# Two attention blocks in one kernel: query blocks of 256 with output and denominator in one PSUM bank, score banks 3+2, a matmul in place of a partition all-reduce, and rearranged loads

## Chip, core, metric

The kernel runs on one core of a Trainium2 chip. The metric is the device time in microseconds (us). A profile is one separate execution, so its span differs a little from the median time. Engines: TensorE (PE; PEld are its weight loads), VectorE (DVE), ScalarE (ACT), GpSimd (POOL); SP issues the DMAs, and SPq is its queue. L392 is a line of the kernel file. The *granted clock* is the share of TensorE's full clock that the chip allowed, as the trace records it.

## The reference

Two independent attention layers over 2048 tokens with 32 heads of 32 channels, in bf16, their outputs set side by side. A is plain softmax attention. B works on four segments of 512 tokens: causal softmax inside the segment, and a memory read from the segments before it.

```python
def _A_ref(x, wqkv, wo):                        # x (1, 2048, 1024)
    q, k, v = ...                               # (x @ wqkv) split into 3 x 32 heads x 32
    p = softmax(einsum('bhqd,bhkd->bhqk', q, k) * 32 ** -0.5)
    return merge_heads(einsum('bhqk,bhkd->bhqd', p, v)) @ wo

def _B_ref(x, wq, wk, wv, wo, beta):            # 4 segments of 512
    g = sigmoid(beta)                           # one gate for each head
    for s in range(4):
        a_dot = softmax(qs @ ks^T * scale + causal mask) @ vs
        a_mem = (phi(qs) @ M) / (phi(qs) @ z + 1e-6)
        outs.append(g * a_mem + (1 - g) * a_dot)
        M, z = M + phi(ks)^T @ vs, z + sum(phi(ks))
    return merge_heads(outs) @ wo
# result: concatenate([A, B], axis=-1)
```

## The kernel before

Heads go in groups of four, since four times 32 channels fill the 128 partitions. For one query block and one tile of 128 keys a *slot* holds the scores of one head, 128 keys by 512 columns, one PSUM bank. ACT takes the exponential of two slots in one call and writes them to a ring `PT` in SBUF. PE then multiplies by V, and by a matrix of ones for the denominators ("PV"). Everything else is *side work* for PE: projections of Q, K and V ("preparation" of a group), output projections, B's memory.

The kernel plans itself. A small simulator in the program books each instruction with a cost, and the order in which it books them is the order in which each engine will run them. The real engines wait for each other by semaphores, in that fixed order. A wrong cost in the plan therefore doesn't make a wrong result, but it can make a poor order.

```python
SLOTS = [(0, 1), (2, 3)]      # score banks, two at a time
PROJ = [4, 5]                 # side work
OB, LB = 6, 7                 # outputs, denominators
...
# in Recorder.op: an operation's end in the plan
t = self.free[eng]
for d in op.deps:
    t = max(t, d.end + LAT)
op.end = t + cost
...
# in b_prep: the shift of B's exponent, one number for all 128 partitions
R.op("PE", f, ...)                                  # sums of squares of q and k
R.op("DVE", lambda e, bank=bank: e.tensor_reduce(self.cbB[b][:, 1:2], self.ps[:, bank, :], AX.X, ALU.max), ...)
R.op("POOL", lambda e: e.partition_all_reduce(self.cbB[b][:, 1:2], self.cbB[b][:, 1:2], P, bass_isa.ReduceOp.max), ..., cost=1.0)
R.op("POOL", lambda e: e.tensor_scalar(self.cbB[b][:, 0:1], self.cbB[b][:, 1:2], -SCALE, None, ALU.mult), ...)
...
# in schedule, at each step of PE's plan: scores if a bank pair is free,
# else a PV step if its exponentials are done, else a piece of side work
if ready and room and self.slot_end[bk] <= now + 0.05:
    self.emit_scores(u, n, bk)
...
if not done:
    for t in self.tasks:
        if t.req[0] == "pe" and self.satisfied(t.req, now, True):
            self.resume(t)
```

## Time and profile before

| | before |
|---|---|
| time, median of 2 runs | 1611.62 us (1604.51 to 1618.72) |
| span of the profiled run | 1628.9 us |
| ACT busy | 1239.1 us |
| PE busy | 1393.8 us, mean granted clock 0.905 |

The profiled run took 1630.61 us, 1.6% above the fastest of the two timed runs (1604.51 us). It is the only profile of before, so the losses read from it are together some 20 us larger than in a run at the median (1630.6 less 1611.6, an estimate).

First the page's table of 40 equal slices of the span (here 40.7 us each). Each digit is the busy share in tenths, and PEclk is the granted clock in tenths of full speed.

```profile
PE   1588999698999987969889998879898997789998
ACT  0228999698789973969769996478888995598970
PEclk9997999798589999979669999688989999998999
```

ACT is saturated in some stretches and starved in others, and the clock dips with it. The next fence cuts the span in three: until the first exponential of A, until the end of the last exponential, and the rest. Columns: the stretch, its length, then busy us (and instructions) of PE, PEld, DVE, ACT and POOL, the granted clock, the share of the DMA engines and GB/s.

```profile
0.00:110.60 110.60, 54.01 (x406) 25.05 (x411) 31.43 (x60) 8.26 (x10) 8.97 (x29) 0.97 0.46 105
110.60:1578.50 1467.90, 1296.64 (x10952) 423.54 (x11090) 738.83 (x1105) 1230.71 (x1240) 142.85 (x315) 0.90 0.11 27
1578.50:1628.90 50.40, 43.12 (x196) 17.76 (x198) 22.04 (x32) 0.09 (x1) 0.00 (x0) 1.00 0.19 69
```

ACT's idle time in a stretch is its length less ACT's busy time: 102.3 us at the start, 237.2 us in the middle, 50.3 us at the end. This is the ledger used below: **span = ACT busy + idle of ACT at the start + in the middle + at the end.** Next, what ACT waited for (total us, times, longest):

```profile
ACT PT L392 <- PE ps L380: 145.8, 136, 30.6
ACT PT L392 <- POOL cbB L615: 87.8, 12, 14.2
ACT E L631 <- DVE KQB L508: 55.0, 6, 18.3
ACT L345 <- DMA beta<-in_B_beta_dram: 50.0, 1, 50.0
```

And two lines of the waits of all engines. "POOL cbB L615 <- issue" is the time that GpSimd stood after issuing the all-reduce: 225.1 us in 32 times, 7.0 us each. In the other, PE waits for causal masks, which GpSimd makes too.

```profile
POOL cbB L615 <- issue: 225.1, 32, 7.6
...
PE ps L444 <- POOL PT L415: 34.6, 5, 12.0
```

What a stop of PE can do to its clock, in stretches of 4 us:

```profile
388.00:392.00 4.00, 3.86 (x51) 1.92 (x49) 0.00 (x0) 4.00 (x5) 0.38 (x1) 1.00 0.02 4
392.00:396.00 4.00, 2.71 (x42) 1.71 (x39) 3.63 (x7) 0.86 (x2) 0.00 (x0) 1.00 0.08 18
396.00:400.00 4.00, 0.30 (x1) 0.14 (x2) 3.86 (x6) 2.12 (x2) 1.09 (x3) 0.76 0.66 146
400.00:404.00 4.00, 3.98 (x27) 0.98 (x26) 0.82 (x2) 3.20 (x4) 1.46 (x3) 0.50 0.44 98
440.00:444.00 4.00, 4.00 (x29) 1.59 (x26) 0.00 (x0) 3.06 (x3) 0.00 (x0) 0.50 0.00 0
456.00:460.00 4.00, 2.95 (x32) 1.34 (x32) 2.98 (x6) 1.46 (x2) 0.53 (x2) 0.99 0.28 64
```

PE has one matmul between 396 and 400; the clock goes to 0.50 and stays there until about 456, though PE is busy for 3.98 and 4.00 of 4 us in the stretches shown, and ACT gets only 3.06 to 3.20 us of work in 4. ACT waits 4.4 us for the shift, until 397.25. PE's next matmul in order is the first projection of the next segment, and the one xB buffer is only now loaded anew:

```profile
394.90 10.39 SPq L293 DMA_TRANSPOSE xB<-in_B_x_dram  x8
...
399.70 0.63 PE L505 MATMUL ps<-xB,WB 128*128 128x512 bf16 x1 [4.92 <-DVE Ls L464]
...
786.62 0.63 PE L505 MATMUL ps<-xB,WB 128*128 128x512 bf16 x1 [4.87 <-DMA xB<-in_B_x_dram]
```

The trace puts the first of these stops down to DVE. In the program this matmul waits for two xB transposes, for weights loaded before and for a bank that DVE freed at 393.0, so xB ended the wait. At the next segment change, which begins the other 60 us of half clock (784 to 844), the trace names xB itself.

### The profile page before, as it was taken

To read this page: it belongs to the slowest core of one execution; us is meant where nothing else is said; L and a number is where in the kernel's file an instruction comes from. 1 tells how busy PE (TensorE), PEld (TensorE's weight loads), DVE (VectorE), ACT (ScalarE), POOL (GpSimd) and SP (SyncE) were. 2 spreads that over 40 slices of the span, in tenths; PEclk is the share of its full clock that TensorE was granted. 3 is DMA by queue.
4 is the path that set the end of the run, shared out by engine and by line. 5 is a ranking of instruction groups with operands and counts; after the bars stand their busy time and mean duration, and the time that the engine had idled before them with its cause. 6 is when DMAs were issued, how large, how long until landed. Compare 5 with 4: busy or idle time off the path is not lost.

```text
span 1628.9 us, 26663 instructions
## 1 busy us (share of the span) xinstructions
PE 1393.8 (86%) x11550; PEld 466.4 (29%) x11696; DVE 792.3 (49%) x1196; ACT 1239.1 (76%) x1250; POOL 151.8 (9%) x344
## 2 busy tenths in 40 slices
PE   1588999698999987969889998879898997789998
PEld 0241233223223233322223323222332232222223
DVE  0343444353255654645526754545545745463643
ACT  0228999698789973969769996478888995598970
POOL 0000001001011010100101100100101101110100
PEclk9997999798589999979669999688989999998999
DMA  8220001002011001100111101100111001310002
GB/s 167 84 47 7 14 22 39 21 14 46 14 33 27 20 21 46 27 14 21 40 27 28 26 21 27 40 13 20 30 37 33 21 1 27 97 27 7 20 30 75
DMA packets 166742, 54.17 MB, mean 33 GB/s; under 512 B 160480, under 2 KB 160480, under 8 KB 166624
## 3 DMA queue, kind: packets, MB, share of 16 engines
q1 hardware_dynamic: 166624, 52.45, 13.2%
q8 instruction: 92, 1.51, 0.4%
q14 instruction: 26, 0.21, 0.0%
HBM read 35.65 MB, written 8.39 MB: 27 GB/s over the span
## 4 chain that ended last, share of the span: by engine, by line
ACT 57%; PE 23%; issue 8%; DVE 6%; SPq 3%; DMA 2%; POOL 1%; POOLq 0%; ACTq 0%; DVEq 0%
ACT PT L392 56%; PE ps L380 6%; PE ps L444 6%; PE ps L505 5%; PE ps L710 4%; PE ps L522 3%; DVE Ls L464 2%; SPq L293 1%; SPq L306 1%; DMA beta<-in_B_beta_dram 1%; DVE outsb L717 1%; DVE Ls L454 1%; DMA out_dram<-outsb 1%; ACT E L631 1%; DVE cbB L610 1%
## 5 line engine op out<-in xcount | busy, mean ns | idle before, releaser
L392 ACT ACTIVATE PT<-ps,cbA 128x1024 bf16<-128x1024 f32 x1024 | 1050.0, 1197 | 112.9 <-PE ps L380 112.1
L380 PE MATMUL ps<-QA,KA 32*128 32x512 bf16 x2048 | 421.6, 410 | 40.3 <-ACT PT L392 15.3
L392 ACT ACTIVATE PT<-ps,cbB 128x768 bf16<-128x768 f32 (+1 forms) x192 | 175.3, 1039 | 121.7 <-POOL cbB L615 87.8
L444 PE MATMUL ps<-PT,ones 128*32 128x512 bf16 (+3 forms) x2560 | 256.0, 395 | 0.0
L464 DVE RECIPROCAL Ls<-Ls 128x128 f32<-128x128 f32 x256 | 242.2, 946 | 3.6
L380 PEld LDWEIGHTS ps<-QA,KA 32*128 32x128 bf16 x2048 | 96.9, 92 | 462.7 <-ACT PT L392 399.0
L444 PE MATMUL ps<-PT,VA 128*32 128x512 bf16 x2048 | 216.4, 413 | 0.9 <-DVE Os L455 0.4
L505 PE MATMUL ps<-xB,WB 128*128 128x512 bf16 x472 | 147.7, 417 | 53.6 <-DMA xB<-in_B_x_dram 18.2
L505 PE MATMUL ps<-xA,WA 128*128 128x512 bf16 x459 | 141.7, 405 | 29.5 <-DMA xA<-in_A_x_dram 18.9
L415 POOL TENSOR_SCALAR_AFFINE_SELECT PT<-PT 128x256 bf16<-128x256 bf16 (+1 forms) x192 | 95.2, 498 | 472.1 <-ACT PT L392 469.2
L380 PE MATMUL ps<-KQB 32*128 32x128 bf16 (+3 forms) x512 | 65.9, 335 | 50.6 <-ACT PT L392 48.2
L454 DVE COPY Ls<-ps 128x512 f32<-128x512 f32 x64 | 44.0, 687 | 107.4 <-PE ps L444 106.8
L508 DVE CAST KQB<-ps 128x512 bf16<-128x512 f32 x64 | 43.6, 681 | 102.1 <-PE ps L505 102.1
L527 DVE CAST VA<-ps 128x512 bf16<-128x512 f32 x32 | 21.8, 682 | 146.5 <-PE ps L522 146.5
L657 DVE RECIPROCAL den<-den 128x128 f32<-128x128 f32 x96 | 91.3, 951 | 2.5
L444 PEld LDWEIGHTS ps<-PT,VA 128*32 128x32 bf16 x2048 | 53.0, 93 | 129.5 <-issue 120.8
L717 DVE CAST outsb<-ps 128x512 bf16<-128x512 f32 x64 | 43.5, 685 | 84.1 <-PE ps L710 72.0
L522 PE MATMUL ps<-WA,xA 128*128 128x128 bf16 x1024 | 82.5, 231 | 0.8 <-DVE VA L527 0.8
L522 PE MATMUL ps<-WB,xB 128*128 128x128 bf16 x1024 | 79.1, 230 | 1.7 <-DVE KA L508 0.5
L444 PE MATMUL ps<-PT,VB 128*32 128x256 bf16 (+3 forms) x512 | 45.9, 356 | 35.6 <-POOL PT L415 34.6
L710 PE MATMUL ps<-WoB,OTB 128*128 128x512 bf16 x237 | 68.3, 403 | 7.8 <-DVE PKt L678 2.6
L505 PEld LDWEIGHTS ps<-xB,WB 128*128 128x128 bf16 x512 | 40.8, 101 | 107.8 <-issue 67.2
(70 smaller groups left out, 900.1 us busy)
## 6 DMA issues: line engine op xcount, KB each, us to landing
WB<-in_B_wk_dram SPq DMA_DIRECT2D x32, 256.0 KB, 2.9
WB<-in_B_wq_dram SPq DMA_DIRECT2D x32, 256.0 KB, 2.9
WB<-in_B_wv_dram SPq DMA_DIRECT2D x32, 256.0 KB, 2.9
out_dram<-outsb SPq DMA_DIRECT2D x32, 256.0 KB, 2.0
WA<-in_A_wqkv_dram SPq DMA_DIRECT2D x24, 256.0 KB, 2.9
WoB<-in_B_wo_dram SPq DMA_DIRECT2D x1, 2048.0 KB, 17.6
xA<-in_A_wo_dram SPq DMA_DIRECT2D x1, 2048.0 KB, 9.5
xB<-in_B_x_dram SPq DMA_TRANSPOSE x32, 2.8
```

The lines of the kernel that those rows point to most:

```text
L380: ins = e.matmul(o, l, r, start=True, stop=True)
L392: op = R.op("ACT", lambda e: e.activation(self.PT[:, s0:s0 + n, 0:width], self.ps[:, banks[0]:banks[0] + n, 0:width], ACTF.Exp, bias=cb, s ...
L415: mo = R.op("POOL", lambda e, ap=ap, pat=pat: e.affine_select(ap, ap, pattern=pat, compare_op=ALU.is_ge, fill=0.0, base=0, channel_multipl ...
L444: ins = e.matmul(o, l, r, start=(st == 0), stop=stop)
L454: R.op("DVE", lambda e: e.tensor_copy(self.Ls2[x][:, :], self.ps[:, LB, :]), r=[("ps", LB)], w=[("Ls", x)], cost=0.66)
L464: R.op("DVE", lambda e, cs=cs: e.reciprocal(Ls[:, cs], Ls[:, cs]), r=[("Ls", x)], w=[("Ls", x)], cost=0.9)
L505: ins = e.matmul(self.ps[:, bank, :], W[:, i, :], xsl(i), start=(i == 0), stop=(i == NI - 1))
L508: op = R.op("DVE", lambda e: e.tensor_copy(dst, self.ps[:, bank, :]), r=[("ps", bank)], w=[dkey], cost=0.66)
L522: ins = e.matmul(self.ps[:, bank, P * t:P * t + P], xsl(i, t), W[:, i, :], start=(i == 0), stop=(i == NI - 1))
L657: R.op("DVE", lambda e, cs=cs: e.reciprocal(self.den[:, cs], self.den[:, cs]), r=["den"], w=["den"], cost=0.9)
L710: ins = e.matmul(self.ps[:, bank, :], lhsT, rhs, start=(j == 0), stop=(j == NG - 1))
L717: op = R.op("DVE", lambda e, ns=ns, bank=bank, ob=ob: e.tensor_copy(self.outsb[ob][:, ns], self.ps[:, bank, :]), r=[("ps", bank)], w=[("ou ...
```

## The change

Its intent: shorter query blocks (256) let output and denominator share one bank, so that two banks fall free; one goes to the scores, where ACT and PE now work on three and two slots in turn. The all-reduce of the shift leaves GpSimd: `col_max` puts the maximum of each partition, made negative, on a diagonal, a matmul with ones copies the diagonal's values to all partitions, and DVE takes the smallest. The plan gets truer costs (a change of tiling on PE costs 0.105 us), starts side work only if it fits before the next score burst ("room"), and lets B run ahead. xA is loaded in quarters so that work can start with the first, the second segment's xB has a buffer of its own and is loaded at once, and the beta gate no longer heads DVE's queue.

```diff
-QC = 512
+QC = 256
+DRAIN = 0.105
+MM = 0.213
-SLOTS = [(0, 1), (2, 3)]
-PROJ = [4, 5]
-OB, LB = 6, 7
+SLOTS = [(0, 1, 2), (3, 4)]
+OLB = 5
+PROJ = [6, 7]
+LEAD = 1.5
...  # loads
-        for i in range(NI):
-            src = self.A_x[0][:, P * i:P * i + P]
-            R.dma(... self.xA[:, i, :], src, transpose=True),
-                  w=[("xA", i)], issue=2.3, cost=3.0)
+        for c in range(4):
+            for i in range(NI):
+                src = self.A_x[0][512 * c:512 * c + 512, P * i:P * i + P]
+                R.dma(... self.xA[:, i, 512 * c:512 * c + 512], src, transpose=True),
+                      w=[("xA", i, c)], issue=0.6, mb=0.125)
+            ...  # beta after c == 0
+        self.load_xB(1)
         R.dma(... self.WoB ...)
...  # emit_scores: each slot is two key tiles by 256 queries
...  # emit_pv: one tile of 128 keys; ones go to columns 256:512 of the same bank
...  # the shift: partition_all_reduce becomes
+    def col_max(self, bank, i, mul, out, okey):
+        dg = self.diag[i]
+        R.op("DVE", ... e.tensor_reduce(out, self.ps[:, bank, :], AX.X, ALU.max) ...)
+        R.op("DVE", ... e.tensor_scalar(dg, self.ident, out, mul, ALU.mult, ALU.mult) ...)
+        R.op("PE",  ... e.matmul(self.ps[:, bank, 0:P], self.ones, dg, start=True, stop=True) ...)
+        R.op("DVE", ... e.tensor_reduce(out, self.ps[:, bank, 0:P], AX.X, ALU.min) ...)
...  # side work in runs as long as there is room
+    def mm_run(self, mms, r, w, each, k0=1):
+        while i < len(mms):
+            room = yield ("pe", 0)
+            k = max(k0, min(len(mms) - i, int((room - DRAIN) / each)))
...  # proj_tok, the V projection, books each matmul at
+        yield from self.mm_run(mms, ..., [("ps", bank)], 0.079, 5)
...  # schedule
+                        late = max(R.free["ACT"] - self.score_cost(u, n) - DRAIN - 0.25, self.slot_end[bk])
+                        room = late - now
```

## The prediction

> **What bounds it now.** ScalarE (ACT), in quiet stretches: the windows have ACT busy 99.99 of 100 us at 200-300 and 98.64 at 900-1000, at clock 1.00. Over the span ACT is busy 1239 of 1629 us, so some 390 us are idle:
> 1. About 105 us before softmax of A runs steadily (first A exponential at 110.6 us). The timeline shows VectorE blocked to 51.5 us behind the gate of beta (ACT waited 50.0 us for that DMA), with evictions queued behind it.
> 2. About 50 us tail: last exponential ends at 1578.5.
> 3. About 235 us in the middle. In the waits, the partition all-reduce holds each B shift some 7 us ("POOL cbB from issue": 225.1 us, 32 times); 87.8 us reach ACT directly. Masks behind it are late (PE waits up to 12.0 us for POOL PT), and the three segment changes starve ACT (4 of 20 us busy at 1000-1020). After these stops the granted clock is 0.50 for up to 55 us (400-456, 792-840) although PE is busy 4.00 of 4 us, and ACT falls to about 75%. The Trainium skill ("TensorE: Matmul & The Clock Gate", What's actually happening) gives half clock after one idle window of about 3.4 us; the trace agrees. It also gives full clock after one busy window; here return took far longer.
>
> **Removed, added.** Estimates from trace durations.
> - ACT: back-to-back 1024-wide exponentials start every 0.994 us (64 in 63.63); 256 elements cost 0.213 us, so about 0.14 us is fixed. A: 1024 calls become about 832 (13 per block of 32 slots): 1018 to 991 us, -27. B about -5. New ACT total about 1180-1200 us.
> - PE, occupied time at full clock from successive starts (a switch of tiling costs about 0.1 us): a score burst 0.32 us for two heads, and with three heads of 2x256 columns about the same: 1024 to 832 bursts, -60. PV per pair of key tiles unchanged (0.46 plus switch). Longer projection runs save perhaps 40 of 107 us of switches; the shift's small matmuls add about 10. Sum about 1340 to 1250 us.
> - POOL all-reduce out of the path: removes its waits and most half-clock stretches.
> - DVE: one 0.69 us copy per 256 block instead of two per 512; the same 242 us of reciprocals; about +25 us for shifts. Not a limit.
> - Second xB buffer: segment changes hidden. Beta moved: prologue loss 105 to about 50 us. Smaller output pieces: tail 50 to about 25 us.
>
> **On the critical path.** 1190 ACT + 50 prologue + 25 tail = 1265. But in the middle PE then needs about 97% of ACT's time, so I add 85 us for semaphore latencies, late scores, and a few half-clock stretches. Predicted 1350 us, range 1270 to 1440. Chances: faster 0.97, same 0.02, slower 0.01.
>
> **What would show it.** ACT A exponentials about 832, busy near 1010-1020; ACT total near 1200 and over 87% of the span; no partition all-reduce and no ACT wait on cbB over 2 us; mean clock 0.95 or more; first A exponential by about 65 us; last one within 35 us of the end; PE busy over 88%.
>
> **What would make it wrong.** More half-clock: attention alone uses only about 60% of PE, and at 116-122 us before, a stretch of attention without side work dropped the clock. Then PE binds: 1400 or more. Or the single output bank stalls PV at each of 128 block ends behind DVE's queue. Or PE blocks in order on xA pieces in the prologue.

## More of the kernel before

Last, the DMA queue at the start (start, duration and number of the issues):

```profile
2.58 10.75 SPq L293 DMA_TRANSPOSE xB<-in_B_x_dram  x8
...
15.44 20.00 SPq L306 DMA_TRANSPOSE xA<-in_A_x_dram  x8
```

Eight transposes of 512x128 for xB took 10.75 us of the queue, and eight of 2048x128 for xA took 20.00 us.

## The result

| | before | after |
|---|---|---|
| time, median of 2 runs | 1611.62 us | 1447.13 us (1445.71 to 1448.56) |
| span of the profiled run | 1628.9 us | 1444.0 us |
| ACT busy | 1239.1 us | 1200.8 us |
| mean granted clock | 0.905 | 0.974 |
| ACT idle at the start | 102.3 us | 119.9 us |
| ACT idle in the middle | 237.2 us | 63.5 us |
| ACT idle at the end | 50.3 us | 59.8 us |

The ratio of after to before is 0.8979 (95% interval 0.8805 to 0.9154). A ratio here is the mean time of one kernel's fast runs over that of the other's of the same rounds, so it isn't quite the ratio of the medians. A later set of four runs of the same kernel gave 1446.44 us and 0.8937. The change is faster, but the range of the prediction ended at 1440 us. The same slices, now of 36.1 us:

```profile
PE   2448999999989899989898889898999999999997
ACT  0104999999999999999869879599999999999930
PEclk9669999999999999999999999999999999999999
```

From the fifth slice on ACT is nearly always full, and the clock is 0.9 or more everywhere past the start. The first three slices are nearly empty. The three stretches:

```profile
0.00:133.60 133.60, 63.02 (x493) 29.38 (x498) 41.20 (x84) 13.70 (x16) 9.48 (x25) 0.81 0.44 95
133.60:1384.20 1250.60, 1138.71 (x17733) 529.62 (x17910) 760.75 (x1271) 1187.12 (x1030) 104.68 (x186) 0.99 0.13 31
1384.20:1444.00 59.80, 49.96 (x252) 22.00 (x252) 26.28 (x40) 0.00 (x0) 0.15 (x1) 1.00 0.18 66
```

What ACT waited for; the wait for cbB is gone:

```profile
ACT PT L417 <- PE ps L405: 123.9, 28, 24.0
ACT gcol L370 <- DMA beta<-in_B_beta_dram: 36.2, 1, 36.2
ACT E L661 <- DVE KQB L547: 21.0, 1, 21.0
```

The start is *longer* than before. The DMA queue shows why:

```profile
1.92 10.51 SPq L306 DMA_TRANSPOSE xB<-in_B_x_dram  x8
...
15.57 10.95 SPq L322 DMA_TRANSPOSE xA<-in_A_x_dram  x8
...
28.67 35.48 SPq L322 DMA_TRANSPOSE xA<-in_A_x_dram  x24
64.19 11.82 SPq L306 DMA_TRANSPOSE xB<-in_B_x_dram  x8
76.06 0.59 SPq L333 DMA_DIRECT2D WoB<-in_B_wo_dram  x1
76.76 0.51 SPq L299 DMA_DIRECT2D WB<-in_B_wk_dram  x1
```

The 32 quarter transposes take 10.95 + 35.48 = 46.4 us in place of 20.0, and then come eight more for the second segment (11.8 us) and the 2 MB of WoB, all ahead of the weights of the *second B block*, issued at 76.76. PE runs in order, so it stands behind them; the first line is ACT's first exponential, the second PE's first matmuls that need those weights:

```profile
62.16 3.26 ACT L417 ACTIVATE PT<-ps,cbB 128x1152 bf16<-128x1152 f32 x3 [22.96 <-PE ps L405]
...
86.60 1.03 PE L537 MATMUL ps<-xB,WB 128*128 128x512 bf16 x2 [17.10 <-DMA WB<-in_B_wk_dram]
```

xB of the first segment had landed by 14 us, yet its first exponential comes at 62 us: A's projections of the quarters stand in front of B's in PE's program, each waiting for its quarter (30.0 us in 4 waits). In the middle the remaining gaps are of one kind, an exponential waiting for scores whose preparation is late:

```profile
732.53 5.37 ACT L417 ACTIVATE PT<-ps,cbB 128x1152 bf16<-128x1152 f32 x5 [14.30 <-PE ps L405]
...
917.19 7.42 ACT L417 ACTIVATE PT<-ps,cbA 128x1536 bf16<-128x1536 f32 x6 [16.44 <-PE ps L405]
```

At the end PE runs five output blocks of A (7.1 us each) and then the last of B (14 us), with short pauses; three of these lines:

```profile
1393.32 7.08 PE L537 MATMUL ps<-xA,OTA 128*128 128x512 bf16 x32 [0.59 <-DVE outsb L743]
1400.56 7.08 PE L537 MATMUL ps<-xA,OTA 128*128 128x512 bf16 x31 [0.16 <-DVE outsb L743]
...
1426.55 13.99 PE L537 MATMUL ps<-WoB,OTB 128*128 128x512 bf16 x63 [3.48 <-DVE OTB L511]
```

### The profile page after: what moved, and what is told of

Its sections match the earlier page's. It is cut to its first block, busy times and chain, and to the rows that moved or that the text cites. A ratio compares the mean times of both kernels' runs of the same rounds, so it can differ in the third digit from the quotient of the medians.

```text
span 1444.0 us, 40280 instructions
## 1 busy us (share of the span) xinstructions
PE 1251.7 (87%) x18472; PEld 581.0 (40%) x18656; DVE 828.2 (57%) x1393; ACT 1200.8 (83%) x1046; POOL 114.3 (8%) x211
## 4 chain that ended last, share of the span: by engine, by line
ACT 72%; PE 16%; SPq 5%; DVE 5%; DMA 1%; issue 1%; POOL 0%; DVEq 0%
ACT PT L417 71%; PE ps L537 11%; SPq L322 3%; PE ps L405 3%; PE ps L466 2%; SPq L306 2%; ACT E L661 1%; DVE OL L486 1%; DMA WB<-in_B_wk_dram 1%; DVE outsb L743 1%; DMA out_dram<-outsb 0%; DVE den L687 0%; DVE OL L476 0%; DVE SQB L636 0%; DVE cbB L564 0%
## 5 line engine op out<-in xcount | busy, mean ns | idle before, releaser
L417 ACT ACTIVATE PT<-ps,cbA 128x1024 bf16<-128x1024 f32 (+1 forms) x832 | 1012.1, 1369 | 60.3 <-PE ps L405 59.9
L405 PE MATMUL ps<-QA,KA 32*128 32x256 bf16 x4096 | 324.3, 273 | 56.3 <-ACT PT L417 44.1
L466 PE MATMUL ps<-PT,ones 128*32 128x256 bf16 (+1 forms) x4864 | 309.8, 271 | 0.0
L466 PE MATMUL ps<-PT,VA 128*32 128x256 bf16 x4096 | 270.8, 279 | 4.0 <-issue 1.8
L486 DVE RECIPROCAL OL<-OL 128x128 f32<-128x128 f32 x256 | 242.4, 948 | 5.0
L417 ACT ACTIVATE PT<-ps,cbB 128x768 bf16<-128x768 f32 (+4 forms) x179 | 174.8, 1073 | 64.6 <-PE ps L405 63.9
L437 POOL TENSOR_SCALAR_AFFINE_SELECT PT<-PT 128x256 bf16<-128x256 bf16 (+2 forms) x147 | 86.1, 596 | 1089.7 <-ACT PT L417 1088.4
L466 PEld LDWEIGHTS ps<-PT,VA 128*32 128x32 bf16 x4096 | 106.6, 94 | 133.6 <-issue 124.3
L476 DVE COPY OL<-ps 128x512 f32<-128x512 f32 x128 | 86.7, 677 | 99.9 <-PE ps L466 99.3
L466 PEld LDWEIGHTS ps<-PT,ones 128*32 128x32 bf16 x4864 | 129.3, 96 | 1.3
L743 DVE CAST outsb<-ps 128x512 bf16<-128x512 f32 x64 | 43.4, 682 | 58.2 <-PE ps L537 50.4
L405 PE MATMUL ps<-KQB 32*128 32x256 bf16 (+1 forms) x768 | 63.2, 257 | 12.1 <-ACT PT L417 8.4
L537 PEld LDWEIGHTS ps<-WB,xB 128*128 128x128 bf16 x1024 | 60.2, 100 | 18.7 <-issue 16.5
```

The source lines that it names most:

```text
L405: ins = e.matmul(o, l, r, start=True, stop=True)
L417: op = R.op("ACT", lambda e: e.activation(self.PT[:, s0:s0 + n, 0:width], self.ps[:, banks[0]:banks[0] + n, 0:width], ACTF.Exp, bias=cb, s ...
L437: mo = R.op("POOL", lambda e, ap=ap, pat=pat: e.affine_select(ap, ap, pattern=pat, compare_op=ALU.is_ge, fill=0.0, base=0, channel_multipl ...
L466: ins = e.matmul(o, l, r, start=start, stop=end, skip_group_check=True)
L476: R.op("DVE", lambda e: e.tensor_copy(self.OL[x][:, :], self.ps[:, OLB, :]), r=[("ps", OLB)], w=[("OL", x)], cost=0.66)
L486: R.op("DVE", lambda e, Lq=Lq: e.reciprocal(Lq, Lq), r=[k], w=[k], cost=0.87)
```

## The experiments

Every experiment is the kernel named with one edit, checked against the reference. Differences in us are from 1447 us of after unless another kernel is named. They go across jobs and chips: e1 to e4, e5 to e8, and e9, e10 and after again were three jobs. After itself gave 1447.1 and 1446.4 us in two jobs. The kernel before, run beside each, gave medians of 1610.9 to 1623.3 us. The ratios use fast runs only: of the kernel before some runs (1629 to 1645 us), and of e5 two of four (1545 and 1548 us), lay over 1.5% above their fastest and count as slow; every run of the other kernels was fast, and so was every profiled run but that of before (see above). Most edits also change the plan, and with it the order of PE's whole program; where that matters I compared the sequences of matmuls by shape. The ledger of the profiled runs, worked out as above:

| kernel | median us | ratio to before | start | middle | end | ACT busy |
|---|---|---|---|---|---|---|
| before | 1611.6 | 1 | 102.3 | 237.2 | 50.3 | 1239.1 |
| after | 1447.1 | 0.8979 | 119.9 | 63.5 | 59.8 | 1200.8 |
| e1 second segment later | 1422.3 | 0.8826 | 98.4 | 49.9 | 74.1 | 1200.1 |
| e2 xA in eight pieces | 1417.9 | 0.8794 | 94.4 | 52.2 | 70.5 | 1200.2 |
| e3 V booked at its time | 1410.1 | 0.8749 | 117.7 | 47.3 | 43.3 | 1201.8 |
| e4 all-reduce back | 1498.8 | 0.9299 | 125.9 | 105.6 | 62.7 | 1203.9 |
| e5 before, matmul shift | 1538.1 | 0.9502 | 94.4 | 141.9 | 49.4 | 1231.0 |
| e6 score banks 2+2 | 1532.6 | 0.9554 | 120.4 | 108.9 | 77.6 | 1226.3 |
| e7 = e1 + e2 + e3 | 1378.7 | 0.8591 | 84.4 | 46.5 | 41.7 | 1201.2 |
| e8 = e7, no standing | 1368.9 | 0.8527 | 75.6 | 43.8 | 43.3 | 1200.8 |
| e9 = e8, half of V (wrong) | 1330.2 | 0.8218 | 71.2 | 18.0 | 38.5 | 1201.3 |
| e10 = e8, lead and margin | 1358.4 | 0.8389 | 76.1 | 30.8 | 47.3 | 1202.8 |

**My first theory after the result**: three losses that add. The start is lost to a serial DMA queue and to PE standing in order behind it; middle and end are PE's side work done too late. **The rival**: PE has more work than the time holds, so that whatever is saved at the start only comes back as backlog.

### e1: the second segment's load and WoB moved out of the start

```diff
-        self.load_xB(1)
-        R.dma(... self.WoB ...)
...
+        if n == 1:              # in b_prep, behind the second B block's loads
+            self.load_xB(1)
+            self.R.dma(... self.WoB ...)
```

> The kernel after, with the second segment's eight transposes of xB and the 2 MB load of WoB moved out of the start, behind the preparation of the second B block. In the trace of after they stand in the one DMA queue before the weights of the second B block, which land at 86.6 us, and TensorE waits 17.1 us in order for them. Theory (the start is lost one for one): 17 to 24 us less, about 1424 us, first A exponential near 113 us instead of 134. Rival (TensorE has more work than the rest of the time holds, so the start only moves the backlog): under 5 us less.

Measured: 1422.27 us, 25 us less; first A exponential at 118.2 us. The start gave 21.5 us of it. The middle gave 14 us, and 14 us came back at the end. That looks like backlog moving on, but it isn't shown to be: e2 has the same shift (11 us each way), and the programs of e1 and e2 have the same sequence of matmuls, which differs from that of after. The rival's "under 5 us" is out, and e7 below repeats the test with the order almost kept.

### e2: xA in eight transposes

```diff
-        for c in range(4):
-            for i in range(NI):   ... 512x128 pieces, w=[("xA", i, c)], issue=0.6, mb=0.125
+        for i in range(NI):
+            src = self.A_x[0][:, P * i:P * i + P]
+            R.dma(... self.xA[:, i, :], src, transpose=True),
+                  w=[("xA", i, c) for c in range(4)], issue=2.5, mb=0.5)
```

> The kernel after, with xA loaded by eight transposes of 2048x128 as before in place of 32 of 512x128. In the traces the eight took 20.0 us of the queue, the 32 took 46.4 us (1.3 us each). Theory (each transpose costs the queue a time of its own, little of it by bytes): the first A exponential comes 20 to 26 us earlier and the kernel is 18 to 26 us faster, about 1423 us. Rival (bytes are what counts, or the early first quarter of xA is worth as much): within 5 us.

Measured: 1417.90 us, 29 us less, a little more than expected; first A exponential at 114.1 us. The queue in this run:

```profile
15.84 20.77 SPq L321 DMA_TRANSPOSE xA<-in_A_x_dram  x8
```

20.77 us for the same bytes that took 46.4 us in quarters. Having the first quarter early was worth less than the queue time it cost. The edit also moves the beta gate behind all of xA (ACT waits 46.3 us for it in place of 36.2).

### e3: one number of the plan

```diff
-        ... [("ps", bank)], 0.079, 5)
+        ... [("ps", bank)], 0.0575, 5)
```

> The kernel after, with one number of its scheduler changed: a 128-column projection matmul of V is booked at 0.0575 us in place of 0.079 us. The trace starts 32 of them in about 1.8 us (0.056 each); 2048 of them are over-booked by 46 us. Theory (TensorE has room in the middle, but the order of its program holds side work back, so preparations come late and output projections pile up at the end): 30 to 50 us less, of it 15 to 25 us of the tail after the last exponential (62 us in after), the rest of gaps of ScalarE in the middle. Rival (TensorE is really full): under 5 us less.

Measured: 1410.05 us, 37 us less, the largest of the three, with no instruction taken away. The end gave 16.5 us and the middle 16.2 us. The plan thought that PE had no room for side work where the chip had it. So at least this part was not lack of PE time but the order.

### e4: the all-reduce back

```diff
-        yield from self.col_max(bank, 1, -SCALE, self.cbB[b][:, 0:1], ("cbB", b))
+        ... DVE tensor_reduce, POOL partition_all_reduce, POOL tensor_scalar, as before
```

> The kernel after, with the shift of B again by the partition all-reduce of GpSimd (about 7 us of delay each, 32 times, in the trace of before). Theory of the prediction (the all-reduce made the middle loss of before, by waits of ScalarE and half-clock stretches after them): 60 us slower or more, mean clock below 0.95, ScalarE waiting over 50 us for cbB. Rival (with two blocks of lead and other work to do, the 7 us are hidden, and the gain in the middle came from the pacing and banks): under 20 us slower.

Measured: 1498.80 us, 52 us more, between the two expectations. The all-reduce stands as long as ever, 7.0 us each, but reaches ACT less often than before:

```profile
POOL cbB L650 <- issue: 224.5, 32, 7.8
...
ACT PT L417 <- POOL cbB L650: 48.0, 3, 19.1
```

42 us of the loss are in the middle; the mean clock is 0.957. One thing is untested here: the plan books the all-reduce at 1.0 us, as it does in before, while it stands 7.0. No run booked it at its time, so some of its cost may be the order and not the wait itself.

### e5: the kernel before with the matmul shift alone

The edit is the same four operations as in `col_max`, in the kernel before, for B only.

> The kernel before with one part of the change alone: the shift of B by two small matmuls and VectorE in place of GpSimd's partition all-reduce (A keeps its own, eight in all). Theory of the prediction (most of the 237 us that ScalarE idles in the middle of before come from the all-reduce and the half clock after it): 80 to 160 us faster than before, 1450 to 1530 us, mean clock 0.95 or more. Rival (putting it back into the kernel after cost only 52 us, so it is worth about that here too, and the rest of the middle loss is one-ahead preparation, segment loads and pacing): 30 to 65 us faster, about 1560 us.

Measured: median 1538.08 us (1518.77 to 1547.92) with two slow runs in it; by the fast runs the ratio is 0.9502 (0.9403 to 0.9602), 82 us less (1524.98 for 1607.14, the means of the fast runs). That is the lower edge of what my theory expected, but with two fast runs the interval (64 to 96 us) reaches down to the rival's 65. The middle went from 237.2 to 141.9 us and the clock of the whole run from 0.905 to 0.957 between the profiled runs; these two differ by more than the medians do, since both kernels spread over some 30 us from run to run. So the all-reduce, alone, is worth some 82 us in the kernel before and 52 us in the kernel after, about a third of the 237 us, most of which I had put on it and the half clock after it. The other 142 us of the middle belong to something else: e6 shows one part.

### e6: score banks 2+2

```diff
-SLOTS = [(0, 1, 2), (3, 4)]
+SLOTS = [(0, 1), (2, 3)]
```

> The kernel after with score banks 2+2 in place of 3+2, the fifth bank left idle. Theory (fewer, longer exponentials and score bursts are the gain of the banks): ScalarE busy 27 to 35 us more in 1024 calls for A, TensorE some 190 more bursts of 0.32 us, kernel 45 to 90 us slower. Rival (neither engine is tight enough for it to show): under 15 us slower.

Measured: 1532.62 us, 85 us more. ACT is busy only 25.5 us more; the rest is 45 us in the middle and 18 us at the end, where PE's side work now comes late. PE's burst for two heads takes as long as that for three. These lines of after show it: six matmuls for three heads start at 704.15 and PE's next starts at 704.48, and the four for two heads start at 710.75, PE's next at 711.07.

```profile
704.15 0.39 PE L405 MATMUL ps<-QA,KA 32*128 32x256 bf16 x6
704.48 0.29 PE L466 MATMUL ps<-PT,VB 128*32 128x256 bf16 x4
...
710.75 0.39 PE L405 MATMUL ps<-QA,KA 32*128 32x256 bf16 x4
711.07 0.29 PE L466 MATMUL ps<-PT,VA 128*32 128x256 bf16 x4
```

So 1024 bursts in place of 832 cost PE 192 x 0.32 = 61 us, an estimate from these distances; the traces have A's score matmuls busy for 399.7 us in place of 324.3. The banks were worth more than any other part tried in the kernel after. I had counted 27 us for ACT and 60 us for PE, but only ACT's part is a term of the predicted sum. e6 also has four banks to fill ahead in place of five, which I didn't separate from the number of bursts.

### e7 and e8: the repairs together, and no standing in order

e7 is e1, e2 and e3, with the queue's measured times in the plan (1.3 and 2.5 us for a transpose, and 0.45 us in place of 0.1 for most other loads). e8 adds to e7, in both projection helpers:

```diff
+        yield ("t", max(self.R.lastw[k].end for k in [wkey] + [xkeys(i) for i in range(NI)]))
         bank = yield ("bank",)
```

> The three repairs e1, e2 and e3 together (second segment and WoB later, xA in eight transposes, V booked at 0.0575 us), and the scheduler told the DMA queue's times of the trace (1.3 us a 512x128 transpose, 2.5 us a 2048x128 one). Alone they gave 25, 29 and 37 us. Theory (start and tail are separate losses that add, e1 and e2 overlapping in part): 65 to 90 us faster than after, 1357 to 1382 us. Rival (they all draw on the same slack): 1395 us or more.

> e7 and one more thing: no projection is put into TensorE's program before the scheduler expects its inputs to have landed, so that TensorE does not stand in order before a load while the first B block could go on. In the trace of after TensorE waited 30 us for xA, and the first exponential came at 62 us though xB had landed by 14 us. Theory (standing in order is part of the start's loss): the first exponential before 35 us, 8 to 20 us faster than e7. Rival (the start is bound by the queue alone): within 5 us of e7.

Measured: e7 1378.67 us, 68 us less than after. Alone the three gave 25 + 29 + 37 = 91 us, so they add only in part. The cleanest pair is e3 and e7: the two sequences of matmuls agree in 16,462 of 18,656 places, the start falls by 33 us (117.7 to 84.4), middle and end by 1 and 2, and the kernel by 31 us. So what the loads cost at the start is lost one for one, and no backlog takes it back. e8 1368.87 us, 10 us less than e7, the first exponential at 25.0 us and the first of A at 89.4 us (103.5 in e7). The expectation of e8 held.

### e9: half of the V projections left out (a wrong result)

```diff
-        mms = [(..., i == 0, i == NI - 1) for t in range(4) for i in range(NI)]
+        mms = [(..., i == 0, i == 3) for t in range(4) for i in range(4)]
```

> e8 with half of the contraction of the V projections left out, a wrong result on purpose: 1024 of 2048 matmuls of 128 columns, 57 us of TensorE spread over the whole run, ScalarE's work the same. Theory (past the start, TensorE's work fills the time: the 44 us of ScalarE's gaps in the middle and the 43 us of tail are its backlog): 35 to 57 us faster than e8. Rival (ScalarE and the waits between the two set the pace): under 15 us faster.

Measured: 1330.24 us, 39 us less than e8 (of another job), for 57 us (an estimate, 1024 x 0.056) of PE's work taken out; the result is wrong. ACT did the same work. Here are the middle stretches of e8 and of e9:

```profile
89.40:1320.10 1230.70, 1174.29 (x18005) 534.99 (x18004) 774.40 (x1296) 1186.88 (x1036) 106.38 (x192) 0.99 0.14 34
85.00:1290.30 1205.30, 1103.36 (x16907) 486.61 (x17100) 776.27 (x1299) 1187.29 (x1038) 107.18 (x194) 0.98 0.15 35
```

ACT's idle time in the middle falls from 43.8 to 18.0 us. So more than half of what is left there is PE's work, and the rival is right about this remainder though it was wrong about the start.

### e10: more lead for B, less margin

```diff
-LEAD = 1.5
+LEAD = 2
-   late = max(R.free["ACT"] - self.score_cost(u, n) - DRAIN - 0.25, self.slot_end[bk])
+   late = max(R.free["ACT"] - self.score_cost(u, n) - DRAIN - 0.15, self.slot_end[bk])
```

> e8 with B blocks allowed two instead of one and a half ahead of A, and 0.10 us less margin kept before a score burst, so that side work is started in smaller remainders of time. Expected: ScalarE's gaps in the middle down by 10 to 20 us, tail up by less; 5 to 12 us faster than e8. If the margin is needed on the chip, scores come late and it is no faster.

Measured: 1358.42 us (1356.25 to 1358.71), correct, 10 us less than e8 (of another job), as expected: the middle fell by 13 us and the end grew by 4. It is 88 us faster than the kernel after in the same rounds (1446.44) and the fastest correct kernel. Its waits of ACT, to set beside those of after:

```profile
ACT PT L413 <- PE ps L401: 61.8, 21, 17.8
ACT E L662 <- DVE KQB L544: 22.9, 2, 16.3
ACT gcol L366 <- DMA beta<-in_B_beta_dram: 19.2, 1, 19.2
```

### after again

> The kernel after, unchanged, to stand beside the next two and to give more runs of it: 1440 to 1452 us.

Measured: 1446.44 us (1445.54 to 1448.10), as expected.

## Why the prediction was wrong

The predicted 1350 us was a sum of four terms; the profile of after gives each one.

| term | predicted | measured | miss |
|---|---|---|---|
| ACT busy | 1190 | 1200.8 | +11 |
| start ("prologue loss 105 to about 50 us") | 50 | 119.9 | +70 |
| middle ("so I add 85 us") | 85 | 63.5 | -22 |
| end ("tail 50 to about 25 us") | 25 | 59.8 | +35 |
| sum | 1350 | 1444.0 | +94 |

- **The step that failed first is "Beta moved: prologue loss 105 to about 50 us".** It priced one removed wait and didn't price the loads that the diff adds to the same queue. The number lay in the trace of before: 10.75 us for eight 512x128 transposes, 1.3 us each. Forty of them more (32 for xA, 8 for the second segment) in place of eight long ones make 52 us less 20 us; the trace of after shows 58.2 us. e1 and e2 took 21.5 and 25.5 us off the start, and with e8 it is 75.6 us, still not 50; what holds the rest I didn't take apart. I had named PE's standing in order behind xA as a risk, and it came true; but I had left it out of the sum.
- **The second is "Smaller output pieces: tail 50 to about 25 us".** The pieces were smaller but didn't come earlier: 220 output matmuls are recorded behind the last exponential in after, 188 in before. e3 shows that 16.5 us of the end were an over-booked cost in the plan. The rest is PE's work at the end of the run, which nothing here removed (38.5 us even in e9).
- **The middle was right in size for a partly wrong reason.** Gone are the wait for cbB and most of the half clock, as predicted. But the 85 us was an allowance for several small losses, not a sum of measured ones, so that it came near is partly luck. And "Longer projection runs save perhaps 40 of 107 us of switches" was too high: counted in the two instruction streams, runs of side work fell from 616 to 530, and all changes of tiling from 2453 to 2303, worth some 15 us at 0.1 us each. And e4 and e5 put 52 and 82 us on the all-reduce, not most of the 237 us. The banks (e6, 85 us) carried more than I gave them.
- **What held**: 832 exponentials of A, busy 1012.1 us (predicted 1010-1020); ACT's total near 1200 us; no partition all-reduce; clock above 0.95; DVE not a limit (828 us busy). What failed: ACT's share (83% for over 87%), the first A exponential (133.6 us for 65) and the last exponential (59.8 us before the end for 35). PE's share (87% for over 88%) isn't decided, since the trace of after lacks records (904 of the 1024 projection matmuls of 512 columns that e6 shows). Of the named risks, the single output bank cost PE 2.5 us of waits ("PE ps L466 <- DVE OL L476").
- **Left open**: of the 142 us that remain in the middle of e5, I haven't separated what segment loads, preparation only one block ahead and the remaining half-clock stretches cost. Nor is it shown what set off the half clock. In stretches of 4 us it was below 0.9 for 352 us in before, 156 in e5 and 100 in after, so the all-reduce probably has a part in it. But the two longest stretches of before begin where PE waits for a new segment's xB, at 120 us it fell with no PE pause over 0.62 us, and e5 kept such a stop (4.8 us at 726) with only 8 us of lower clock. No run varied a stop alone.

## What to carry to other kernels

Before pricing what a change removes from a start, price what it adds to the same in-order queue: cutting a load into quarters cost more queue time (46 us for 20) than the earlier first quarter was worth. In a kernel that plans its own order, a cost that is wrong by 0.02 us per instruction cost 37 us with no engine doing less work, so check each booked cost against the distance of starts in the trace. And keep a ledger of the bounding engine's idle time by start, middle and end: the sum says at once which term of a forecast failed.

## What the Trainium skill lacked or had wrong

- "TensorE: Matmul & The Clock Gate", section What's actually happening: half clock after an idle window of about 3.4 us agrees with the trace of before (a pause of 4.92 us up to 399.70, then 0.50). But the clock fell without one too (0.70 from 120 to 124 us, after pauses of at most 0.62 us). Full clock after one busy window of about 3.4 us didn't come here: 0.50 stood from 400 to 456 us with PE busy at least 3.67 of every 4 us. What counts as busy for the clock, no run here separates.
- "GPSIMD Engine Reference", section When to use GPSIMD, names GpSimd as the only option for a reduction over partitions. Here an all-reduce of 128x1 stood 7.0 us, and a maximum over partitions by DVE, one matmul of ones with a diagonal, and DVE took 2.1 us from the first reduction's start to the last one's end (99.54 to 101.60 us in the trace of after). The page gives 247,699 ns for a `tensor_reduce` of 128x2048 over the partitions and no time for so small a reduction.
- "DMA: Bandwidth & Descriptors", section DMA Transpose (X-bar), gives no time in the queue for a transpose by its size (a table elsewhere on the page has sequencer cycles of earlier chips for small tiles, without the transfer). Measured: 1.3 to 1.8 us for 512x128 (eight in 10.51 us in after, in 14.75 us in e2) and 2.5 to 2.8 us for 2048x128 (eight in 20.00 us in before, in 22.10 us in e8), one after the other.
- "TensorEngine Tiling (Array Packing)", Key Properties, says that changing the tiling mode drains TensorE but not what it costs. Here a score burst of 512 columns took 0.32 us from its start to the next start, while 32 side matmuls of 512 columns took 7.08 us, 0.22 each, so a change costs about 0.1 us.
